# Strassen's products in a weight fold, sums of q one stage earlier, and PSUM split by phase

## The chip, the cores and the metric

One core of one Trainium2 chip. The metric is the device time of one execution in microseconds (us), median of several executions. Times in profile lines count from the start of the span. An execution counts as slow when it lies over 1.5% above the fastest of the same kernel; ratios use the fast ones. One execution of each version keeps a trace; where that is a slow one, the text says so. "The clock" is the clock that was granted to TensorE, as a share of full speed.

## The reference, cut to what matters

```python
q_lm = q.reshape(B, H, 32, S // 32, D).mean(axis=3)      # B, H, S, D = 8, 8, 576, 64
k_lm = k.reshape(B, H, 32, S // 32, D).mean(axis=3)
A, Bm, C = sm(q, k_lm), sm(q_lm, k_lm), sm(q_lm, k)      # softmax of scaled products
Z = Bm^T / (norm1(Bm) * norminf(Bm) + 1e-6)
for _ in range(6):
    Z = 2 * Z - Z @ Bm @ Z
x = (A @ Z @ C @ v)                                      # -> 4608 x 512
h = (x @ w1) * (x @ w2) @ w3                             # w1, w2: 512 x 1024; w3: 1024 x 1024
out = h @ w_out                                          # w_out: 1024 x 512
```

The kernel multiplies w3 by w_out once (the "fold") and so has one product less per token.

## The kernel before

There are two regions. In the first 82.5 us TensorE folds w3 into w_out, with the attention of batch 0 in between. Then come eight rounds, one per batch: an **up** phase (x times w1 and w2, with the next batch's attention woven in by stages) and a **down** phase (times the folded weight, with what is left of that attention, the Newton chain of Z). The attention is a generator; each `yield` ends a stage, and the loop decides where a stage is issued. What is issued on an engine behind a wait comes after it: in the changed kernel TensorE stood 11.2 us for v at L283, and the fold's products issued behind that began only afterwards, at 60.7.

PSUM: three tiles of two banks in turn (`big`), one bank `small`, one bank `acc`.

```python
def big():
    return psp.tile([128, 2, 512], FP32, name="big", bufs=3)
...
def attention(st, bank=None, vbank=None):
    combine(st, 0)                 # lm of q = sum of two halves, on VectorE
    nc.vector.tensor_tensor(out=qbd, ...)               # block diagonal of it
    psB = small()                  # Bm's scores: first use of lm on TensorE
    ...
    yield
    scores_c(0); es0 = presum(0)   # on GpSimd (POOL)
    combine(st, 1)                 # lm of k, used by scores_a two stages on
    yield
    ...                            # Newton: six iterations, then
                y = pz.tile([128, 2, 32], FP32, name="y")
                nc.vector.tensor_tensor(out=y, in0=old[:, :, 2, :], in1=pv_[:, :, 1, :], op=ALU.add)
                ybd = pz.tile([128, 2, 4, 32], FP32, name="ybd")
                nc.vector.tensor_tensor(out=ybd, in0=y..., in1=mask4..., op=ALU.mult)
    ...
    psZ = small()                  # ybd is the moving operand of this product
```

The fold and its loads (order of issue is what matters):

```python
for n, (j, cc) in enumerate(blocks):          # 16 half row blocks of w3
    # transpose four 128x128 pieces on TensorE, copy to SBUF, then
    nc.tensor.matmul(psW[j][:, :], turned[j, cc][:, c4, :], wof[:, c, :], ...)   # 512 columns
...
fd = fold(pf, wof, w3f)
steps(fd, 5)
load_w3(3)
turn_all(0)                                   # transposes of q and k, batch 0
steps(load_v(sts[0], 0), 9)                   # v of batch 0
...
load_weight(0, moe_w1); load_weight(1, moe_w2)
steps(load_qk(sts[1], 1), 9)
```

The softmax here doesn't subtract the row's maximum and nothing guards it: scores larger than these inputs give would overflow.

## Time and profile before

| | kernel before |
|---|---|
| median time | 296.25 us (295.93 to 298.0, 3 runs) |
| profiled span | 293.7 us, of an execution of 295.47 us; granted clock 0.997 |
| first up product (L437) | 82.5 us |
| from there to the end | 211.2 us |
| waits of TensorE for the sums of q (L197) | 2.2 us by the view of waits |

Two stretches make the time: up to the first up product, which I call the **fold region**, and the **rounds** after it.

### The profile page before, as it was taken

The page shows a single profiled execution, that of the slowest core. Times are in us where ns is not written, and L with a number is a line of the kernel's source. Part 1 is how long each engine was busy: PE and PEld are TensorE (multiplying, and loading weights), DVE is VectorE, ACT ScalarE, POOL GpSimd, SP SyncE. Part 2 cuts the span into 40 slices and gives each one's busy share as a digit, 9 for nine tenths or more (in the row PEclk, how much of TensorE's full clock was granted, in tenths as well). Part 3 has the DMA queues.
Part 4 walks back from the last instruction along what each step waited for, and adds up shares of the span by engine and source line. Part 5 has one row for each costly group of instructions (what it writes and reads, how often), then busy time and mean ns, then how long its engine had stood idle before and what let it go on. Part 6 is the DMA issues. An engine that isn't in the chain of part 4 may idle for free.

```text
span 293.7 us, 8702 instructions
## 1 busy us (share of the span) xinstructions
PE 279.8 (95%) x3632; PEld 155.3 (53%) x3632; DVE 168.7 (57%) x416; ACT 127.3 (43%) x209; POOL 130.7 (45%) x157
## 2 busy tenths in 40 slices
PE   7999998989999999999999999999999999999994
PEld 4444454444466546654664565466546645654741
DVE  7111145434048678665876786586678657975620
ACT  1000026994164257225723742474257236625531
POOL 0208805078029906950794299049807910400000
PEclk9999999999999999999999999999999999999998
DMA  6999999999915889896999799979979365003124
GB/s 230 337 251 205 242 261 206 176 215 207 157 27 69 147 260 167 123 254 187 145 133 280 177 147 166 294 137 141 187 230 148 91 164 158 2 21 90 37 52 126
DMA packets 69127, 48.80 MB, mean 166 GB/s; under 512 B 40672, under 2 KB 61152, under 8 KB 69088
## 3 DMA queue, kind: packets, MB, share of 16 engines
q1 hardware_dynamic: 54208, 34.62, 49.3%
q0 software_dynamic: 13792, 11.54, 27.5%
q10 hardware_dynamic: 1088, 2.10, 1.9%
q8 instruction: 28, 0.46, 0.6%
q14 instruction: 11, 0.09, 0.1%
HBM read 38.80 MB, written 9.44 MB: 164 GB/s over the span
## 4 chain that ended last, share of the span: by engine, by line
PE 82%; DVE 7%; ACT 5%; DMA 3%; issue 2%; ACTq 0%; DVEq 0%
PE big L437 20%; PE acc L511 13%; PE acc L457 11%; PE big L457 9%; PE small L511 5%; PE small L273 5%; PE big L423 4%; DVE ab L443 3%; PE small L365 3%; PE acc L365 3%; DMA wof<-in_moe_w_out_dram 3%; DVE gt L429 2%; PE small L399 2%; PE big L479 2%; ACT gt L427 1%
## 5 line engine op out<-in xcount | busy, mean ns | idle before, releaser
L437 PE MATMUL big<-ahat,gt 128*128 128x288 f16 x512 | 74.3, 286 | 0.8
L443 DVE TENSOR_TENSOR ab<-a_sb,big 128x576 f16<-128x576 f16 x64 | 48.1, 752 | 25.1 <-PE big L437 11.3
L441 ACT CAST a_sb<-big 128x576 f16<-128x576 f32 x64 | 40.8, 638 | 37.6 <-PE big L437 37.6
L437 PEld LDWEIGHTS <-gt 128*128 128x128 f16 x512 | 46.5, 97 | 18.2 <-issue 2.2
L511 PE MATMUL acc<-wof,w3t 128*128 128x512 f32 x96 | 46.8, 608 | 2.1 <-ACT w_79 L514 1.1
L457 PE MATMUL acc<-w_79,ab 128*128 128x512 f16 (+1 forms) x192 | 40.9, 381 | 0.0
L457 PEld LDWEIGHTS <-ab 128*128 128x128 f16 (+1 forms) x320 | 24.9, 100 | 29.1 <-issue 7.3
L154 POOL TENSOR_TENSOR tr<-qkT 128x768 f32<-128x768 f16 x16 | 26.4, 1649 | 24.2 <-DMA qkT<-qkn 24.0
L457 PE MATMUL big<-w_79,ab 128*128 128x512 f16 x128 | 32.3, 381 | 0.0
L429 DVE TENSOR_SCALAR gt<-big 128x512 f16<-128x512 f32 x32 | 20.6, 687 | 20.0 <-ACT gt L427 20.0
L463 ACT ACTIVATE o_sb<-acc 128x512 f32<-128x512 f32 x20 | 11.9, 598 | 42.1 <-PE acc L457 41.1
L156 POOL TENSOR_TENSOR tr<-tr,qkT 128x768 f32<-128x768 f32 x16 | 26.4, 1652 | 0.4
L511 PEld LDWEIGHTS acc<-wof,w3t 128*128 128x128 f32 x96 | 16.3, 190 | 16.4 <-issue 11.9
L487 DVE COPY w3t<-big 128x512 f32<-128x512 f32 (+1 forms) x15 | 8.5, 583 | 28.2 <-PE big L479 28.2
L427 ACT ACTIVATE gt<-big 128x512 f16<-128x512 f32 x32 | 17.8, 596 | 6.9 <-PE big L423 6.9
L463 ACT ACTIVATE o_sb<-big 128x512 f32<-128x512 f32 x16 | 9.6, 598 | 21.3 <-PE big L457 20.4
L423 PE MATMUL big<-wdup,zt 128*32 128x512 f16 x256 | 17.6, 382 | 0.8 <-DVE zt L406 0.5
L273 PE MATMUL small<-vt,ect 96*32 96x64 f32 x672 | 15.5, 223 | 0.6 <-issue 0.6
L92 ACT COPY wdup<-wdup 64x1024 f16<-64x1024 f16 x16 | 15.4, 1040 | 0.1
L514 ACT CAST w_79<-acc 128x512 f16<-128x512 f32 x6 | 3.5, 586 | 27.2 <-PE acc L511 27.2
L511 PE MATMUL small<-wof,w3t 128*128 128x512 f32 x32 | 14.7, 593 | 0.0
L221 ACT ACTIVATE ect<-big 96x768 f32<-96x768 f32 x16 | 12.9, 808 | 1.6 <-PE big L217 1.6
(148 smaller groups left out, 342.8 us busy)
## 6 DMA issues: line engine op xcount, KB each, us to landing
vt<-in_v_dram SPq DMA_DIRECT2D x24, 288.0 KB, 4.4
out_dram<-o_sb SPq DMA_DIRECT2D x24, 192.0 KB, 2.6
qkn<-in_q_dram POOLq DMA_DIRECT2D x12, 288.0 KB, 5.7
qkn<-in_k_dram POOLq DMA_DIRECT2D x12, 288.0 KB, 6.1
w3f<-in_moe_w_dram SPq DMA_DIRECT2D x6, 512.0 KB, 8.6
out_dram<-o_sb SPq DMA_DIRECT2D x24, 128.0 KB, 3.4
vt<-in_v_dram SPq DMA_DIRECT2D x2, 1152.0 KB, 9.2
wof<-in_moe_w_out_dram ACTq DMA_DIRECT2D x4, 512.0 KB, 7.7
```

What stands on the lines that cost most here:

```text
L154: nc.gpsimd.tensor_tensor(out=tr, in0=x[:, :, 0, :], in1=x[:, :, 1, :], op=ALU.add)
L156: nc.gpsimd.tensor_tensor(out=tr, in0=tr, in1=x[:, :, 2, :], op=ALU.add)
L273: nc.tensor.matmul(psV[32 * h:32 * h + 32, 0:64], ects[qd][0:NP, h, r, :], vt[0:NP, 4 * qd + h, 64 * r:64 * r + 64], start=(r == 0), stop= ...
L423: nc.tensor.matmul(psG[32 * h:32 * h + 32, n, :], zt[:, 4 * qd + h, :], wdup[:, 4 * qd + h, w, 512 * n:512 * n + 512], start=True, stop=Tr ...
L427: nc.scalar.activation(out=dst[:, 0, :], in_=psG[:, 0, :], func=AXF.Copy, scale=1.0 / ZS)
L429: nc.vector.tensor_scalar(out=dst[:, 1, :], in0=psG[:, 1, :], scalar1=1.0 / ZS, scalar2=None, op0=ALU.mult)
L437: nc.tensor.matmul(p[:, c, 0:HS], st["g"][qd][:, w, 128 * j:128 * j + 128], st["ahat"][qd][:, c, :], start=(qd == 0), stop=(qd == 1))
L441: nc.scalar.copy(out=st["a_sb"], in_=p[:, :, 0:HS])
L443: nc.vector.tensor_tensor(out=st["ab"][:, j, :].rearrange("p (c s) -> p c s", c=2), in0=st["a_sb"], in1=p[:, :, 0:HS], op=ALU.mult)
L457: nc.tensor.matmul(pso[o:o + sz, :], ab[:, j, s0:s0 + sz], w34[:, j, :], start=(j == 0), stop=(j == 7), tile_position=(0, o))
L463: nc.scalar.activation(out=o_sb, in_=pso[:, :], func=AXF.Copy, scale=1.0 / (X64 * X64))
L511: nc.tensor.matmul(psW[j][:, :], turned[j, cc][:, c4, :], wof[:, c, :], start=(c == 0), stop=(c == 7))
```

## The change

Its intent: row blocks 2 to 7 of the fold, in pairs, with Strassen's seven products instead of eight; the sums of q a stage ahead of Bm, so that Bm's scores do not wait; copies of w1 and w2 to the other 64 partitions ("doubling") half on VectorE; the iterations of the Newton chain further apart in the fold (`slots`); and PSUM split so that the fold gets banks of its own and the rounds get `third` and `acc` in their place. To find room, three rows of w3 and the sums of w_out lie in the two buffers of v, so v of batch 0 is loaded later. The diff, cut to its core:

```diff
+    ps_fold = tc.tile_pool(name="psf", bufs=1, space=bass.MemoryType.PSUM)
+    ps_late = tc.tile_pool(name="psl", bufs=1, space=bass.MemoryType.PSUM)
     def big():
-        return psp.tile([128, 2, 512], FP32, name="big", bufs=3)
+        turns["n"] += 1
+        if psl is not None and turns["n"] % 3 == 0 and not turns["held"]:
+            return third()
+        return psp.tile([128, 2, 512], FP32, name="big", bufs=2)
+    def third():
+        return psl.tile([128, 2, 512], FP32, name="third")
@@ attention: a stage boundary behind the sums of q, combine(1) later
+        yield
         psB = small()
         ...
         scores_c(0)
         es0 = presum(0)
-        combine(st, 1)
         yield
         ...
         nc.vector.transpose(out=bt, in_=bm)
+        combine(st, 1)
         yield
@@ fold: rows 0 and 1 as before; sums of w_out; then per pair of rows
+                if n == 2 and c4 == 0:
+                    put(s4, wb[1][0], wb[0][0], ALU.subtract, nc.gpsimd)
+                    put(s1, wb[0][0], wb[1][1], ALU.add, nc.gpsimd)
+                if n == 2 and c4 == 2:
+                    put(s6, wb[0][0], wb[0][1], ALU.add)
+                if n == 3 and c4 == 0:
+                    put(wb[0][1], wb[0][1], wb[1][1], ALU.subtract)
+            for i, (a, rhs) in enumerate(products):          # seven
+                m = psf.tile([128, 256], FP32, name="mm", bufs=2)
+                for c in range(4):
+                    nc.tensor.matmul(m, cur[a][:, c, :], rhs[:, c, :], ...)
+                ...                                          # sums of products on VectorE
@@ loads
+        w3x, sums = (pin.tile([128, H, 384], FP32, name="vt")... for _ in range(2))
         turn_all(0)
-        steps(load_v(sts[0], 0), 9)
         landmarks(sts[0])
         load_weight(0, moe_w1)
         load_weight(1, moe_w2)
         steps(load_qk(sts[1], 1), 9)
         exchange(sts[0], 0)
         exchange(sts[0], 1)
+        steps(fd, 16)
+        load_w3(7)
         for n in range(28):
-            steps(at)
+            if n == 0:
+                steps(load_v(sts[0], 0), 9)
+            if n in slots:
+                steps(at)
-                double_weight(0, 2 * n - 7)
+            if 12 <= n < 20:
+                double_weight(nc.vector.tensor_copy, 1, n - 12)
@@ rounds
+            if n == nd - 4:
+                at = attention(sts[b + 2], acc) if b + 2 < B else iter(())
+                steps(at)
```

## The prediction

> **What bounds the kernel now.** I read the page first (busy times and groups), then the timeline of the first 100 us, then the waits, then the DMA packets. The page:
>
> ```profile
> span 293.7 us, 8702 instructions
> ...
> PE 279.8 (95%) x3632; PEld 155.3 (53%) x3632; DVE 168.7 (57%) x416; ACT 127.3 (43%) x209; POOL 130.7 (45%) x157
> ...
> L511 PE MATMUL acc<-wof,w3t 128*128 128x512 f32 x96 | 46.8, 608 | 2.1 <-ACT w_79 L514 1.1
> ...
> L511 PE MATMUL small<-wof,w3t 128*128 128x512 f32 x32 | 14.7, 593 | 0.0
> ```
>
> PE is busy 95% of the span, and the first fold lines say what the change attacks: w3 times w_out, L511, is 128 PE records for 64 matmuls in the source, since each f32 matmul is two passes. The profiled span is 293.7 us and the timed median 296.25, so I add 2.55 us to a span to get a time.
>
> The timeline gives the true cost of a pass:
>
> ```profile
> 12.09 2.74 PE L511 MATMUL small<-wof,w3t 128*128 128x512 f32 x6
> ...
> 30.16 0.60 PE L479 MATMUL big<-ident,w3f 128*128 128x128 f32 x4
> 30.60 4.46 PE L511 MATMUL small<-wof,w3t 128*128 128x512 f32 x10
> ...
> 60.37 0.61 PE L399 MATMUL small<-ybd,xd 128*128 128x128 f32 x4
> ```
>
> Ten passes take 4.46 us, of which the last shows its full 0.59: (4.46 - 0.59)/9 = 0.430 us from start to start. The fold so holds PE for 128 x 0.430 = 55.0 us, 41.3 of it for row blocks 2 to 7. L399, f32 with 128 columns and a fresh weight load each time, goes at (0.61 - 0.275)/3 = 0.112 us, so a 128x128 f32 weight load can repeat every 0.11 us and stays hidden behind a pass of 256 columns.
>
> Where PE waits, from the groups of waits and from the starts in the timeline:
>
> ```profile
> PEld L197 <- DVE lm L174: 4.1, 6, 0.8
> ...
> PE acc L511 <- ACT w_79 L514: 1.1, 2, 0.9
> ```
>
> L197 (Bm's scores) waits at six stage boundaries for the sums of q. From start to start these are 0.444 us three times and 0.630 three times beyond the work, where a plain change of operation costs 0.093. Over the first 82.3 us the fold and attention 0 lose another 3.1 us in seven waits of 0.2 to 1.05 us, the largest where ACT's copy of w34 (L514) stands behind work of its own queue.
>
> [...] at 16.0 to 17.5 us w3 (4096-byte packets, SP queue) ran at about 305 GB/s and k (768-byte packets, POOL queue) at 52, some 37 packets each per half us; alone, k ran at 203. [...] (L487, 512 f32 columns, 0.69 us; lm, 256 columns, 0.42), and I use those two durations.
>
> **The change, part by part.**
>
> 1. Strassen. 3 pairs x 7 products x 4 matmuls = 84 matmuls of 256 columns, 168 passes x 0.2155 = 36.2 us, in place of 96 x 0.430 = 41.3. PE gains **5.0 us** (7/8, as it should be). The 16 transposed groups stay 16. Added on DVE per pair: five sums of 512 (0.69 each) and eight of 256 out of PSUM (0.42), 6.8 us; 20.5 in all, against 8 copies x 0.69 taken away; three sums of w_out on DVE and two on POOL (1024 columns; L154's 1.65 us for 768 makes about 2.2 each). In 24 to 76 us DVE is under half busy, and the two product banks leave 1.7 us per product, so I count these as hidden, with 0.5 us of small stalls (one bank `tr` for all transposes).
>
> 2. Doubling of wdup half on DVE, and slots further apart for the Newton iterations (two fold steps of 0.86 us between them, before mostly one). This should remove about 2 of the 3.1 us of waits. Up to the end of region A (82.3 us now) I get -5.0 - 2.0 + 0.7 = **-6.3 us** if every load is there in time.
>
> 3. Sums of q one stage ahead: 3 x 0.444 + 3 x 0.630 - 6 x 0.093 = **-2.7 us**. PSUM split: the up phase keeps three buffers in turn, the down phase two plus one; it neither adds nor takes a wait that I can point to. One more iteration falls into the up phase, where `small` is held by the product with v; I give 0.4 us back. So **-2.3**.
>
> 4. The loads. Rows 2 to 4 of w3 now lie in one vt buffer and the sums of w_out in the other. So v of batch 0 can be issued only when the last transpose of row 4 is done. I count PE forward: 16 matmuls of rows 0 and 1 end at about 24.0 us (22.4 now, plus three more transposes of 0.43, plus 0.3); 26 more of 0.431 and four transposes put that point at **36.9 us**. The first use of v (L283, in order on PE) comes 12 fold matmuls, two transposes and three attention stages later: 5.2 + 0.9 + 1.9 = 8.0, at **45 us**. Now v is issued at 23.58 and lands at 31.7, in a quiet stretch. After, it stands in the SP queue behind the exchange of k's sums and row 7 of w3, and beside w1, w2, q and k of batch 1 on the POOL queue, which run from about 34 to 57 us:
>
> ```profile
> vt<-in_v_dram SPq DMA_DIRECT2D x2, 1152.0 KB, 9.2
> ...
> wdup<-in_moe_w_dram POOLq DMA_DIRECT2D x2, 1024.0 KB, 13.9
> qkn<-in_q_dram POOLq DMA_DIRECT2D x2, 576.0 KB, 13.1
> qkn<-in_k_dram POOLq DMA_DIRECT2D x2, 576.0 KB, 15.8
> w3f<-in_moe_w_dram SPq DMA_DIRECT2D x4, 256.0 KB, 6.0
> ```
>
> Packets of v are 1536 bytes (0.091 us each), those of w1 and w2 0.172 us: in turn, 16 x 1536 / 0.263 us = 93 GB/s, and 144 beside q and k. 1.18 MB then takes 8 to 12 us. With row 7 ahead of it until about 42 us (the like load, issued at 34.6 now, lands at 43.5), v lands at an estimated **49 to 54 us**. PE then stands 4 to 9 us at L283, and at the long end loses a further 1 us or so to the clock. Central: **+6.5 us**.
>
> Sum: -6.3 - 2.3 + 6.5 = -2.1, span 291.6, time 294.1; I state **293.5 us**, leaning a little toward the shorter wait, since a tuned schedule would hardly keep the longest.
>
> **The rivals.** (a) v arrives in time, as the slots intend: then -8.6, time about 288. For it: v took 8.2 us in its quiet stretch. Against it: the POOL stream is certain to run at that moment, and row 7 must come first. (b) The wait for v takes nearly the whole 9 us and the clock drops: -8.6 + 10 = about 298. For it: the exchange now issued at 33.25, beside the start of w1, needed until 40.7 to land. Against: PE would meet other waits there anyway. (c) DVE becomes the bound of the fold: some 29 us of fold and sum work beside the Newton chain, in order. Then iterations slip by 0.5 us each and the time is about 296. Against: DVE was busy 4.4 to 5.0 us of each 10 between 40 and 70.
>
> **Range and chances.** Rival (a) with some luck gives the lower end, **289.0**, rival (b) the upper, **298.5**. Faster by over 2% means below 290.3: it needs a wait for v under about 3 us, to which I give 0.2. Slower than 302.2 needs two of the rivals at once, 0.05. Within 2%: **0.75**.
>
> **What would show each step.** Product passes (L574) start to start 0.215 us, 168 of them[...]. A wait of L283 for DMA vt of several us at about 45 us, once, in batch 0 alone; none would make me wrong towards faster. The waits of L207 (Bm's scores) at the six boundaries down to about 0.1 us. The stretch from the first up matmul to the end 2 to 3 us shorter than the 211 now. Granted clock below 1.0 after the wait for v[...]. If the fold ends before 77 us, step 4 failed; if DVE lines end PE's waits in the fold, step 1's "hidden" failed.

## More of the kernel before

The prediction shows the lines of the page; one more group matters later, VectorE's write of `ybd` (columns: count, shortest/median/longest ns, first and last start, forms):

```profile
L377 DVE TENSOR_TENSOR ybd<-y,mask_129 x8: 424/432/611, 59.4 to 264.3; 128x256 f32<-128x256 f32 x8
```

## The result, and the profile after

The changed kernel took **314.05 us** median (309.71 to 316.61, 4 runs), the kernel before on the same chip 296.88. The ratio of the mean of one kernel's fast runs to the mean of the other's in the same rounds is 1.0495, 95% interval 1.036 to 1.063; it is not quite the ratio of the medians, and here it rests on two fast runs, since two of the four are slow. The run with the trace is one of these two (314.55 us, span 312.7; the fast ones have spans of 307.6 and 311.5, and all four a mean clock of 0.971 or 0.972), so the losses below are those of a long run: up to 5 us more than in the fastest. Slower by 5%, where I had said 293.5 and at most 298.5.

The page's first line and two others (second line of each quotation: busy time, share, instructions; third: granted clock in tenths, 40 slices):

```profile
span 312.7 us, 8888 instructions
...
PE 278.5 (89%) x3704; PEld 170.3 (54%) x3704; DVE 197.2 (63%) x458; ACT 121.2 (39%) x203; POOL 138.2 (44%) x159
...
PEclk9999996579999999999999999999999999999999
```

TensorE's busy time hardly fell (279.8 to 278.5), although the products became fewer (3.0 us of it are work at half clock, see below), and the clock row has a hole at slices 7 to 9. The first up product (L448 now) comes at 94.9 us instead of 82.5: **12.4 us lost in the fold region**; from there to the end it is 217.8 instead of 211.2: **6.6 lost in the rounds**. The waits of TensorE (what it waited for: us in total, times, longest):

```profile
PE big L283 <- DMA vt<-in_v_dram: 11.2, 1, 11.2
PE third L269 <- DVE lm L183: 2.7, 7, 0.5
PE small L409 <- DVE ybd L387: 2.5, 4, 1.1
PE small L283 <- issue: 2.4, 2, 1.9
PE tr L499 <- DMA w3f<-in_moe_w_dram: 2.2, 1, 2.2
PE small L375 <- DVE chain L381: 1.5, 1, 1.5
...
PE tr L499 <- DVE aop L512: 1.4, 1, 1.4
```

The first line is the one that the prediction's fourth step named. L207, Bm's scores, is gone from the view, as its third step said; but L269 and L409 have come in its place. The timeline of TensorE and of the queue SP that carries the loads:

```profile
47.86 0.63 PE L499 MATMUL tr<-ident,w3f 128*128 128x128 f32 x4 [2.23 <-DMA w3f<-in_moe_w_dram]
...
59.93 0.87 PE L283 MATMUL big<-vt,ect 96*32 96x64 f32 x24 [11.19 <-DMA vt<-in_v_dram]
```

```profile
39.11 0.53 SPq L624 DMA_DIRECT2D w3f<-in_moe_w_dram  x1
39.74 0.38 SPq L90 DMA_DIRECT2D vt<-in_v_dram  x1
```

Row 7 of w3 was issued at 39.1 and landed at 47.7 (TensorE stood 2.2 us for it), v at 39.7 and landed at 59.8: 12.1 us behind the row before it in its queue. w1 and w2, issued just ahead on POOL's queue, landed at 49.4 and 58.6. After the wait the clock stays down (columns of this view: stretch, length, busy us of PE, PEld, DVE, ACT, POOL with counts, granted clock, DMA share, GB/s):

```profile
59.50:66.00 6.50, 6.07 (x58) 4.34 (x59) 2.30 (x8) 2.36 (x3) 0.00 (x0) 0.50 1.31 181
66.00:70.00 4.00, 4.00 (x67) 2.94 (x70) 2.08 (x6) 4.00 (x6) 1.54 (x1) 0.98 1.24 217
```

6.07 us of work at half clock would have been 3.0 at full, so another 3.0 us are lost; from start to start the passes took 0.426 us until 65.9 and 0.216 after. But the half clock did not begin late in the gap of 11.2 us: the clock was at half from 49.1 us on, 0.4 us into the gap and soon after the wait of 2.2 us for row 7:

```profile
48.70:49.10 0.40, 0.04 (x8) 0.00 (x0) 0.00 (x0) 0.40 (x2) 0.40 (x1) 1.00 1.05 211
49.10:59.90 10.80, 0.00 (x0) 0.00 (x1) 0.00 (x0) 1.61 (x3) 0.28 (x1) 0.50 1.16 217
```

Other traces below have stretches of half clock, 3.4 or 6.8 us long, after single pauses of TensorE of only 1.5 us (unshift), 1.7 and 2.2 (v_early_act), 1.8 (best1) and 2.0 (shift_lm), while a pause of 1.6 in best3 and seven of 1.5 in unshift have none. So half clock follows pauses of 1.5 to 2.2 us in some runs and not in others.

The fold region adds up: v 11.2, clock 3.0, row 7 2.2, and 1.4 and 1.5 for VectorE (L499 and L375 above) are +19.3; less 5.1 for the products, as predicted, and the 3.1 of waits that the kernel before has there, +11.1, of 12.4 measured. (These terms are worked out from the views of one slow run; 1.3 us are not traced to a cause.)

Strassen's products themselves went as predicted: 96 + 72 records of line L574, 0.216 us apart at full clock.

The sums of w_out did not go as predicted. The view of their line (count, shortest/median/longest ns, first and last start, forms):

```profile
L512 POOL TENSOR_TENSOR vt<-wof x2: 2361/2848/3336, 16.5 to 18.8; 128x1024 f32<-128x1024 f32 x2
L512 DVE TENSOR_TENSOR wof<-wof x2: 2358/2808/3257, 20.0 to 27.1; 128x1024 f32<-128x1024 f32 x2
L512 DVE TENSOR_TENSOR vt<-wof x1: 2902/2902/2902, 17.0 to 17.0; 128x1024 f32<-128x1024 f32 x1
```

VectorE took up to 3.3 us for a sum of 1024 columns from SBUF. In a run below with no such overlap it took 1.216. The same holds for its copies in the doubling: 0.41 us for the shortest of eight, 2.20 for the longest, beside an add of POOL.

The same view has a group that tells the operands apart. The three `aop<-aop`, with both operands in SBUF, took 0.68 us twice with no POOL instruction beside them, and 2.11 once beside POOL's adds (32.7 to 34.8); the twelve `aop<-tr,aop`, with one operand in PSUM (`tr`), took 0.675 to 0.692, seven of them beside an add of POOL. And of the eight copies the two beside POOL took 2.20 and 0.98 us, the six with nothing of POOL beside them 0.41 to 0.42. So two operands in SBUF beside POOL looked like what stretches a sum on VectorE. I tested it below.

### The profile page after: what moved, and what is told of

It is laid out like the page before. It is cut to its first block, busy times and chain, and to the rows that moved or that the text cites.

```text
span 312.7 us, 8888 instructions
## 1 busy us (share of the span) xinstructions
PE 278.5 (89%) x3704; PEld 170.3 (54%) x3704; DVE 197.2 (63%) x458; ACT 121.2 (39%) x203; POOL 138.2 (44%) x159
## 4 chain that ended last, share of the span: by engine, by line
PE 54%; DVE 9%; issue 3%; ACT 1%; POOL 0%; DVEq 0%; ACTq 0%
PE big L448 14%; PE acc L468 10%; PE third L468 8%; PE big L434 5%; PE small L283 4%; PE third L448 3%; DVE ab L454 3%; PE acc L375 3%; PE small L409 2%; DVE ybd L387 1%; PE third L269 1%; DVE lm L183 1%; PE big L360 1%; PE small L375 1%; DVE chain L255 1%
## 5 line engine op out<-in xcount | busy, mean ns | idle before, releaser
L448 PE MATMUL big<-ahat,gt 128*128 128x288 f16 x408 | 62.1, 287 | 1.2 <-issue 0.7
L448 PEld LDWEIGHTS <-gt 128*128 128x128 f16 x512 | 45.8, 97 | 16.4 <-issue 1.3
L238 POOL TENSOR_TENSOR t<-ect 96x384 f32<-96x384 f32 x16 | 16.0, 997 | 82.1 <-ACT ect L231 54.5
L468 PE MATMUL acc<-w,ab 128*128 128x512 f16 (+1 forms) x192 | 39.7, 381 | 0.0
L468 PE MATMUL third<-w,ab 128*128 128x512 f16 x128 | 32.2, 380 | 0.0
L574 PE MATMUL mm<-wof,aop 128*128 128x256 f32 x96 | 23.5, 386 | 0.0
L574 PE MATMUL mm<-vt,aop 128*128 128x256 f32 x72 | 20.5, 426 | 0.0
L452 ACT CAST a_sb<-third 128x576 f16<-128x576 f32 x16 | 10.2, 638 | 23.9 <-PE third L448 23.9
L574 PEld LDWEIGHTS mm<-wof,aop 128*128 128x128 f32 x96 | 17.4, 190 | 3.1 <-issue 0.8
L283 PE MATMUL small<-vt,ect 96*32 96x64 f32 x672 | 15.8, 223 | 2.4 <-issue 2.4
L448 PE MATMUL third<-ahat,gt 128*128 128x288 f16 x104 | 17.1, 286 | 0.2 <-ACT o_sb L474 0.2
L554 PE MATMUL big<-wof,aop 128*128 128x512 f32 x32 | 15.3, 599 | 1.0 <-DMA wof<-in_moe_w_out_dram 0.5
```

What stands on the lines that cost most here:

```text
L238: nc.gpsimd.tensor_tensor(out=t3[0:NP], in0=e[:, :, 0:3, :], in1=e[:, :, 3:6, :], op=ALU.add)
L283: nc.tensor.matmul(psV[32 * h:32 * h + 32, 0:64], ects[qd][0:NP, h, r, :], vt[0:NP, 4 * qd + h, 64 * r:64 * r + 64], start=(r == 0), stop= ...
L448: nc.tensor.matmul(p[:, c, 0:HS], st["g"][qd][:, w, 128 * j:128 * j + 128], st["ahat"][qd][:, c, :], start=(qd == 0), stop=(qd == 1))
L452: nc.scalar.copy(out=st["a_sb"], in_=p[:, :, 0:HS])
L468: nc.tensor.matmul(pso[o:o + sz, :], ab[:, j, s0:s0 + sz], w34[:, j, :], start=(j == 0), stop=(j == 7), tile_position=(0, o))
L574: nc.tensor.matmul(m, cur[a][:, c, :], rhs[:, c, :], start=(c == 0), stop=(c == 3))
```

## The experiments

All were run as full kernels that give the correct result. A call of four runs shared one chip and its runs of the kernel before: 296.38 us median for the first four runs below in time order (v_early, unshift, shift_only, v_early_unshift), 296.11 for the next four (v_early_act, v_early_sums, v_early_unshift2, best1), 296.95 for qbd_early, shift_lm, shift_ybd and best2, 296.75 for the last two.

### Was it the load of v?

**v_early**: rows 2 to 4 of w3 lie elsewhere, so v of batch 0 is issued where the kernel before issues it. To make room the rows get a third buffer, and the loads of rows 4 and 5 change places; all else is as in the change.

```diff
-        w3x, sums = (pin.tile([128, H, 384], FP32, name="vt")... for _ in range(2))
+        w3f |= {j: pat.tile([128, DF], FP32, name="gt0", bufs=2) for j in (2, 3)}
+        sums = pin.tile([128, H, 384], FP32, name="vt")...
         ...
         turn_all(0)
+        steps(load_v(sts[0], 0), 9)
         ...
         for n in range(28):
-            if n == 0:
-                steps(load_v(sts[0], 0), 9)
```

> The changed kernel with rows 2 and 3 of w3 in the buffers that later hold gt0, a third buffer for the other rows, and v of batch 0 issued right after the transposes of q and k, as before the change. Theory 'late v': the wait of 11.4 us for v, the half clock after it (about 3.5 us in the trace) and part of the wait for row 7 go, so about 15 us less than the changed kernel: 298 to 300 us. Rival 'DVE of the fold' (the sums on DVE and their collisions with POOL set the pace of the fold): PE then waits for DVE in other places and less than 8 us come back, 306 us or more.

Measured 303.22 us median (301.23 to 309.48), 1.0224 of the kernel before (1.0151 to 1.0296): 10.8 us of the median come back, less than the 15 of my theory and more than the 8 of the rival. The wait of 11.2 us and the half clock are gone (clock 1.00 from 40 to 80 us). The first up product comes at 82.4 instead of 94.9, and the rounds stay at 217.4. So 12.5 us of the fold region hang on this load in the two profiled runs. But 82.4 is the time of the kernel before: the 5.1 us of Strassen are not there either. In their place TensorE waits in that region for:

```profile
PE small L409 <- DVE ybd L387: 4.9, 6, 2.0
PE third L269 <- DVE lm L183: 2.5, 7, 0.4
PE tr L499 <- DMA w3f<-in_moe_w_dram: 1.9, 1, 1.9
...
PE tr L499 <- DVE aop L512: 1.4, 1, 1.4
```

(2.0 us of the first line lie in the fold region, at 68.4; the second line is of the rounds.)

**v_early_act**: the doubling all on ScalarE.

```diff
-            if 12 <= n < 20:
-                double_weight(nc.vector.tensor_copy, 1, n - 12)
+            if 12 < n < 21:
+                double_weight(nc.scalar.copy, 1, n - 13)
```

> v_early with all sixteen doublings of wdup on ACT, one per step. In v_early the stretch up to the first up matmul is 82.2 us, no shorter than before, with waits of PE of 2.2 us ahead of the product with ybd and 1.1 in a Strassen product near 68 to 73 us. Theory 'DVE beside POOL': DVE's operations on two SBUF operands, or its fast copies, stand while POOL works on SBUF (one doubling took 2.2 us against 0.42 alone); without the doublings DVE keeps up, 2 to 3 us come back: 300 us. Rival 'ACT queue': the doublings delay ACT's copies of products and zt, as before the change, and nothing or less than 1 us is won.

302.63 us (298.77 to 304.24), 1.0138 (1.0061 to 1.0215): by the time alone not to be told from v_early, whose interval overlaps. Its profiled run is one of the slow ones, with half clock from 48.5 to 55.4 us and from 181.7 to 185.1, so its spans settle nothing. In its trace the wait for `ybd` in the fold region falls from 2.0 to 0.8 us, and the wait of 0.9 for VectorE at 73.5 is gone.

**v_early_sums**: two edits at once. All four first sums of w_out go to POOL, so that none on VectorE lies beside them, and row 7 of w3 is loaded ahead of the second exchange.

```diff
+                    put(s6, wb[0][0], wb[0][1], ALU.add, nc.gpsimd)
+                    put(wb[0][1], wb[0][1], wb[1][1], ALU.subtract, nc.gpsimd)
                     put(s4, wb[1][0], wb[0][0], ALU.subtract, nc.gpsimd)
                     put(s1, wb[0][0], wb[1][1], ALU.add, nc.gpsimd)
-                if n == 2 and c4 == 2:
-                    put(s6, wb[0][0], wb[0][1], ALU.add)
-                if n == 3 and c4 == 0:
-                    put(wb[0][1], wb[0][1], wb[1][1], ALU.subtract)
         ...
         exchange(sts[0], 0)
-        exchange(sts[0], 1)
         steps(fd, 16)
         load_w3(7)
+        exchange(sts[0], 1)
```

> v_early with four of the five sums of w_out on POOL, one after the other (DVE keeps the last), and row 7 of w3 loaded ahead of the exchange of k's sums. Theory 'DVE beside POOL': two DVE sums took 2.9 and 3.3 us beside POOL's 2.4 and 3.3 where an estimate from L154 and lm gives 1.1 to 2.2; the 1.6 us wait for the fourth transpose of the first pair goes; the wait of 2.0 us for row 7 goes with its earlier load. Together 2.5 to 3.5 us less than v_early: 300 us. If the fold waits for POOL's later sums instead, no gain.

300.33 us (296.58 to 302.52), 1.0107 (1.0027 to 1.0188). Its interval overlaps that of v_early, so by the time alone the gain is not shown, and its profiled run is a slow one. In the trace the waits at 23.8 and 45.6 (1.4 and 1.9 us) are gone, and the first up product comes at 79.9, 2.5 earlier than in v_early, in spite of half clock from 67.8 to 71.2; the wait for `ybd` just before it, at 64.8, grew to 3.1 us, behind two copies of the doubling on VectorE that took 1.63 and 2.39 us beside POOL. The one sum left on VectorE now stands alone:

```profile
L512 DVE TENSOR_TENSOR wof<-wof x1: 1216/1216/1216, 25.4 to 25.4; 128x1024 f32<-128x1024 f32 x1
```

1.216 us against 2.36 to 3.26 in the change. The two edits were not separated.

### The rounds: the shift and the banks

**unshift**: the change without the shift of stages; Strassen, loads and banks as in the change.

```diff
-        yield
         psB = small()
         es0 = presum(0)
+        combine(st, 1)
-            if n == nd - 4:
-                at = attention(sts[b + 2], acc) if b + 2 < B else iter(())
-                steps(at)
+        at = attention(sts[b + 2], acc) if b + 2 < B else iter(())
```

> The changed kernel with the sums of q in one stage with Bm again, combine(1) where it was, and the next attention created at the end of the down phase; Strassen and the PSUM split stay. The part after the fold became 6.4 us longer. Theory 'stage shift': the shift did that (combine(1) behind the chain of bt, ybd beside POOL), so about 6 us come back: 308 us. Rival 'PSUM split': the two plus one buffers did it, and the time stays at 312 to 315 or rises by the 2.7 us that the shift was to gain.

321.17 us (318.7 to 322.73), 1.0833 (1.0776 to 1.0890): slower than the change by 7 us, the opposite of what I looked for. The rounds take 226.6 us, of which some 1.7 go to a stretch at half clock (168.8 to 172.3). Seven times TensorE waits for a bank:

```profile
PE third L467 <- DVE rmix L352: 10.7, 7, 1.5
```

L467 is the first down product into `third`. Without the shift, the denominators of the attention (the tile psS, taken by `big()`, and held until VectorE has made `rmix` of it) come, in the turn of three, to lie in `third` when the down phase begins. Before, the down phase took any of three tiles. So the split of PSUM is not neutral: in this kernel **it needs the shift**. **v_early_unshift** is the same with v early.

> Both: v early and no stage shift, so Strassen and the PSUM split without the two suspected losses. If both theories hold, the 5 us of Strassen and some of the removed waits are seen: 288 to 292 us. If the Strassen sums on DVE eat their gain, 295 to 298.

311.87 us (306.27 to 315.42), 1.0378 (1.0320 to 1.0437); both of my expectations missed. Its profiled run is a slow one, and its trace has the same seven waits with the same sum, 10.7 us. **v_early_unshift2** keeps that one tile out of `third`:

```diff
         def denominators():
-            ps = big()
+            ps = psp.tile([128, 2, 512], FP32, name="big", bufs=2)
```

> v_early without the stage shift, and with the tile of the denominators taken from the two buffers of big, never from third. In unshift PE waited 1.68 us per batch at the first down matmul into third, because the denominators held third. Theory 'the split needs the shift': these waits go, and the part after the fold is 211 us as before the change, so 4 to 6 us less than v_early: 297 to 299 us. Rival 'PSUM split costs by itself': waits move to other buffers and the time stays over 302.

297.35 us (296.97 to 306.48), 1.0045 (0.9997 to 1.0092). The seven waits are gone, and the rounds take 213.2 us against 217.4 with the shift. So, once that bank is free, the version without the shift is faster, by some 4 us in these two traces. Not all of it is the shift's own: 2.9 us of v_early's rounds are the pauses that the view calls "issue", against 0.2 here (more on them under qbd_early). **shift_only** looks at this from the other side: the kernel before with the shift alone.

```diff
+        yield
         psB = small()
         es0 = presum(0)
-        combine(st, 1)
         nc.vector.transpose(out=bt, in_=bm)
+        combine(st, 1)
+            if n == nd - 4:
+                at = attention(sts[b + 2], acc) if b + 2 < B else iter(())
+                steps(at)
```

> The kernel before with the stage shift alone (qbd a stage of its own, combine(1) after bt, attention of the next batch begun four steps before the end of the down phase). Theory 'stage shift': 3 to 6 us slower than before, 300 to 303. Rival 'PSUM split' (and the prediction): 2 to 3 us faster than before, 294.

300.17 us (299.6 to 301.09), 1.0135 (1.0103 to 1.0167). The waits at Bm's scores are gone here as well; in their place stand:

```profile
PE small L400 <- DVE ybd L378: 3.5, 4, 1.3
PE big L260 <- DVE lm L174: 2.9, 8, 0.4
PE big L329 <- issue: 1.8, 1, 1.8
...
PE small L274 <- issue: 1.2, 1, 1.2
```

L260 is scores_a: it waits for the sum of k, which the shift put behind the chain of `bt` on VectorE. L400 is psZ. The two pauses ("issue") in which TensorE waits for nothing that the view names were 0.6 each before.

**shift_lm**: combine(1) ahead of the chain of `bt` again.

```diff
+        combine(st, 1)
         rbs = pz.tile([128, 2], FP32, name="rbs")
         ...
         nc.vector.transpose(out=bt, in_=bm)
-        combine(st, 1)
```

> The kernel before with the stage shift (300.2 us in its run), and combine(1) issued ahead of the bt chain again instead of behind it. Theory 'the new 0.47 to 0.57 us waits at scores_a come from the landmark of k being queued behind the bt chain on VectorE': these seven waits go, sum 3.5 us less, about 297. Rival 'VectorE has no room in that stretch, whatever the order': the waits move to the bt chain or to the psZ product, and the time stays within 1 us of 300.

303.32 us (301.97 to 305.21), 1.0232 (1.0160 to 1.0303): my theory fell. The seven waits at scores_a are gone, and the up product waits instead, seven times, for VectorE's product `ab`:

```profile
PE big L438 <- DVE ab L444: 4.3, 7, 0.6
```

The rival was right that the waits move, but it named other places for them, and a time within 1 us of 300. Some 1.7 us of the profiled run are half clock (210.3 to 213.7, after a pause of 2.0). As far as these two orders show, VectorE has no room in that stretch: its order only chooses who waits. That no order would do is not shown.

**qbd_early**: the kernel before, with the sums of q one step early and every later stage left where it was.

```diff
+        yield
         psB = small()
-            steps(proj if n in (nd - 3, nd - 2) else at)
+            if n != nd - 1:
+                steps(proj if n in (nd - 3, nd - 2) else at)
+            if n == nd - 4:
+                steps(at, 9)
+                at = attention(sts[b + 2], acc) if b + 2 < B else iter(())
+                steps(at)
```

> The kernel before with one thing alone moved: the sums of the two q outputs (landmark, block diagonal) of the batch after next are started one up phase step earlier, behind the fourth step from the end instead of the last; all later stages stay where they are, and so does PSUM. The waits of TensorE at the scores_a transposed product (L197 of the kernel before), 3 of 0.44 and 3 of 0.63 us, sum 3.2, go, and nothing takes their place, because combine(1), the Bm sums and the bt chain are not moved. Theory 'the waits are only moved by what the change shifted along': about 2.6 us less, 293.5. Rival 'any shift of the q sums collides with the fold phases or the y chain': within 0.5 us of before, with the waits elsewhere.

299.63 us (299.49 to 301.29), 1.0122 (1.0055 to 1.0188): both expectations missed. The waits of 3.2 us are gone, and the kernel is slower all the same. psZ waits 1.6 us, and one of TensorE's pauses is 3.4 us instead of 0.6, with half clock from 126.0 to 129.4 after it, which is another 1.7 us. These two are 4.4 us over the kernel before, and the span is 4.0 longer (297.7): by this estimate the early sums themselves neither cost nor gain much here. The timeline:

```profile
125.31 0.16 PE L279 MATMUL small<-ones,es 96*32 96x1 f32 x1 [3.36 <-issue]
```

The traces do tell where these pauses stand. The page counts packets that carry instructions (`q8 instruction: 28, 0.46, 0.6%` in the kernel before: 28 packets, 0.46 MB), and the packet records of the trace give the time of each. The 16 traces have 30 pauses over 0.5 us that the view calls "issue". Each ends 1.1 to 1.7 us after such a packet of 16384 bytes has landed; and where this is the k-th packet of the run, the instruction after the pause is TensorE's number 256 k + 193 or 194, in all 30 cases. So, by these counts, TensorE stands there for the instructions that the packet brings, 256 to a packet; the pauses are 0.55 to 3.36 us long. Here the packet began at 122.5 us, in the kernel before at 120.1. What makes a packet late I did not test.

**shift_ybd**: shift_only, with `y` written into PSUM, so that the write of `ybd` has one operand from SBUF and one from PSUM.

```diff
-                y = pz.tile([128, 2, 32], FP32, name="y")
+                y = psI[:, 128:192].rearrange("p (a m) -> p a m", m=32)
```

> The kernel before with the stage shift, and the product y written into PSUM, so that the block-diagonal write ybd has one operand from SBUF and one from PSUM instead of two from SBUF. Theory 'the write of ybd is stretched to 1 us and over because it reads two SBUF operands while POOL adds landmarks': its longest falls from 1.85 to below 0.8 us, the waits at psZ (up to 1.07 us, sum about 4) fall below 0.4 each, and the time is about 297.5. Rival 'it is only late, by the queue in front of it': its duration falls little, or the waits stay, and the time stays at 300.

298.35 us (296.33 to 301.3), 1.0037 (0.9966 to 1.0108), against 1.0135 (1.0103 to 1.0167) of shift_only: the intervals just touch. The rounds took 211.4 us against 214.7 in the two profiled runs; 1.1 of these 3.3 us are a shorter "issue" pause (0.8 for 1.8). The group of the write in shift_only, then here:

```profile
L378 DVE TENSOR_TENSOR ybd<-y,mask x8: 425/660/1849, 60.8 to 267.6; 128x256 f32<-128x256 f32 x8
```

```profile
L378 DVE TENSOR_TENSOR ybd<-small,mask x8: 424/424/425, 60.8 to 264.3; 128x256 f32<-128x256 f32 x8
```

From 425 to 1849 ns down to 424 to 425: the instruction is the same, only the place of one operand moved. And the timeline of shift_only at one of the long ones, POOL then VectorE:

```profile
156.18 1.65 POOL L156 TENSOR_TENSOR tr<-tr,qkT 128x768 f32<-128x768 f32 x1
```

```profile
156.81 1.31 DVE L378 TENSOR_TENSOR ybd<-y,mask 128x256 f32<-128x256 f32 x1
```

POOL's add ends at 157.83, VectorE's write at 158.12. The other two long ones (1.85 and 1.33 us) end 0.28 and 0.29 us after an add of POOL as well, and so do the two of 1.18 and 1.50 us in the change (0.30 and 0.29). That fits a wait until the other is done; work queued in front of the write, the rival, would not tie its end to POOL's. The waits at psZ, 3.5 us in shift_only, are gone from shift_ybd's view of waits.

### A version without the waits

**best1**: all of the above together on the change: v early, four sums on POOL, row 7 ahead of the exchange, the doubling on ScalarE, no shift, psS never in `third`.

> All of it: v early, row 7 early, four sums of w_out on POOL, doublings on ACT, no stage shift, denominators never in third. If the theories hold, the stretch up to the first up matmul falls from 82.2 to about 76 us and the rest stays at 211: 288 to 291 us, faster than both kernels. If 295 or more, another cost of Strassen is still unfound.

296.75 us (294.27 to 298.92), 1.0000 (0.9935 to 1.0066): the case "295 or more" of the expectation. The first up product comes at 74.7 us: 7.8 us gained, Strassen's 5.1 and most of the waits of the fold region. Then the rounds took 222.4. The profiled run is one called slow, so I take its waits as signs only; one is of a kind that had not been there:

```profile
PE small L282 <- DMA vt<-in_v_dram: 3.6, 1, 3.6
```

It is v of batch 1, whose buffer the sums of w_out hold, issued at 76.2 behind the exchanges and landed at 84.3. The fold, now faster, got to it before its load: the same mistake as with batch 0, uncovered by the gain, and again with half clock after it (83.7 to 90.5; the mean of 80 to 90 is 0.68).

**best2** loads that v ahead of the exchanges, starts each up phase with the same turn of the banks, and takes the sums of q one step early as in qbd_early.

```diff
                 landmarks(sts[1], load_qk(sts[2], 2, 4))
+                steps(load_v(sts[1], 1), 9)
                 exchange(sts[1], 0)
                 exchange(sts[1], 1)
-                steps(load_v(sts[1], 1), 9)
                 ...
-        turns["held"] = False
+        turns.update(n=0, held=False)
```

> The change with v of batch 0 ahead of w1 and w2, four sums of w_out on POOL, row 7 of w3 ahead of the exchange, the doubling on ScalarE, the three psS tiles kept out of the bank of the denominators, v of batch 1 loaded ahead of the exchanges of the first batches, and the q sums one step early with the later stages where they were before. The 3.75 us wait for v of batch 1 after the fold goes, so the 7.8 us that the fold gained are kept; the scores_a waits (3 us) go as well. Theory 'the Strassen fold is worth its products once nothing waits for a load': 287 to 290 us. Rival 'the clock gives it back': the span's granted clock is below 0.98 and the time is 293 to 297, with waits as short.

290.97 us (289.33 to 295.45), 0.9792 (0.9727 to 0.9858), clock 0.999. The wait for v is gone, and the first up product stays at 74.8. It beats both kernels: the interval lies below 1, though not wholly below 0.98. **best2_noq** asks whether the early sums of q have a part in that; it is best2 without them.

> The version of 291.0 us without its last part: the q sums stay where the kernel before has them. Theory 'the gain of the fold is kept by loading v of batch 1 ahead of the exchanges': the span's first up product comes at 74.5 us as in the best version, the 3.75 us wait for v is gone, the waits at the scores_a transposed product are back (3.2 us), time 291 to 293. Rival 'the early q sums are the gain': 295 to 297, as the version without either had (296.75).

290.33 us (289.49 to 294.14), 0.9783 (0.9735 to 0.9831): none. The waits for the sums of q are back and the time is the same. Loading v of batch 1 earlier (together with the reset of the turn, not separated from it) makes the difference to best1.

**best3** is best2 with `y` in PSUM, the edit of shift_ybd.

> The version of 291.0 us with the product y written into PSUM, so that the block-diagonal write ybd reads one operand from SBUF and one from PSUM. Theory 'that write is slowed by POOL's adds because it reads two SBUF operands': its longest falls below 0.8 us, the waits at psZ (5 of 0.3 to 0.57 us, sum about 2.2) go for the most part, time 289 to 290. Rival 'what is left of them is other work queued on VectorE': waits and time as in the best version, 291.

287.59 us (287.16 to 291.41), **0.9743** (0.9663 to 0.9824), 9.2 us below the kernel before in the medians. That it is faster than best2 is not shown, for the intervals overlap; in the traces the waits at psZ (1.3 us in best2) are gone, beside others that the edit does not touch. Its page, and its first waits:

```profile
span 285.4 us, 8891 instructions
...
PE 274.7 (96%) x3704; PEld 169.0 (59%) x3704; DVE 183.6 (64%) x448; ACT 127.6 (45%) x211; POOL 140.8 (49%) x161
```

```profile
PE big L338 <- issue: 1.6, 1, 1.6
PE big L634 <- DVE warm L631: 1.5, 1, 1.5
```

TensorE is busy 5.1 us less than before, the size of Strassen's seven for eight (5.0 predicted), and now the span shows it: the first up product at 74.8 (82.5 before), the rounds 210.6 (211.2). No wait for a load is left among the first, and `ybd` takes 423 to 424 ns every time.

The region numbers of the profiled runs together (the change's is a slow run too):

| run | first up product, us | rounds, us | median time, us |
|---|---|---|---|
| before | 82.5 | 211.2 | 296.25 |
| the change | 94.9 | 217.8 | 314.05 |
| v_early | 82.4 | 217.4 | 303.22 |
| v_early_unshift2 | 82.2 | 213.2 | 297.35 |
| best1 (profiled slow) | 74.7 | 222.4 | 296.75 |
| best2 | 74.8 | 214.1 | 290.97 |
| best2_noq | 75.1 | 212.6 | 290.33 |
| best3 | 74.8 | 210.6 | 287.59 |

## Why the prediction was wrong

It was wrong in size and in direction: 293.5 us said, 314.05 measured; slower by over 2% had been given 0.05.

- **Step 4, the load of v: mechanism right, term mis-sized.** The prediction had +6.5 us, with 9 us and "a further 1 us or so" of clock at its long end. Measured: 11.2 us and 3.0 us of clock, and with the load moved back 12.5 us of the fold region are gone (v_early). The slip is in the landing, "49 to 54": v took 12.1 us from the landing of row 7, the top of the 8 to 12 that I had estimated, but row 7 landed at 47.7 and not at "about 42". Its load was no slower than "the like load" before (8.6 us against 8.9); it was issued late, at 39.1. In its queue it stands behind the exchange of k's sums, and POOL had these sums ready at 37.9, where the kernel before has them at 32.7:

```profile
37.06 0.81 POOL L169 TENSOR_TENSOR parts<-parts,tr 128x256 f32<-128x256 f32 x1
```

```profile
31.91 0.80 POOL L160 TENSOR_TENSOR parts<-parts,tr 128x256 f32<-128x256 f32 x1
```

POOL began its sums 4.0 us later (26.7 against 22.7; k had landed at 24.3 against 20.3, with more rows of w3 loading beside it; whether they delayed it I did not test), and two of its adds took 2.5 and 2.0 us for 1.6. I had kept the times of this queue from the kernel before. That TensorE came to L283 at 48.7 and not at 45 was luck and hid 3.7 us of it. Nor did I ask what a row 7 that late does to its own user: TensorE waited 2.2 us for it. And I named the clock, but the 1 us that I gave it was an estimate that no trace then at hand showed; at half clock for 6 us it is 3.
- **Step 1, Strassen: the products right, "hidden" wrong.** The 168 passes ran 0.216 us apart at full clock, and the 5 us are real in best3. But I counted the sums of w_out at 2.2 us each, from POOL's adds, with three on VectorE and two on POOL, as if the engines did not meet. They slowed each other (up to 3.3 us on VectorE, which alone takes 1.2), and a wait of 1.4 us for VectorE ended in the transposes of the first pair. The test that the prediction itself gave, "if DVE lines end PE's waits in the fold, step 1's 'hidden' failed", came out so.
- **Step 2, the doubling: failed in the same way.** Copies on VectorE took up to 2.2 us beside POOL's sums of k and q, in front of the Newton chain in VectorE's queue; in v_early this is the wait of 2.0 us at 68.4. In the changed kernel's own trace it is the wait of 1.5 us for the chain (L375), with copies of 2.20 and 0.98 us just ahead of it on VectorE. What the step was to take away in waits came back there.
- **Step 3, the shift: the waits that it named are gone, the gain is not.** I predicted -2.3 us in the rounds; they became 6.6 us longer. I subtracted a wait without asking what else moved: combine(1) went along, behind the chain of `bt`, and scores_a waits 2.7 us for it; the last product of the Newton chain came to stand beside POOL's adds, and psZ waits 2.5. The change's "issue" pauses are longer as well (3.1 us in three, 1.2 in two before). shift_only has all of these without Strassen, at +3.8 us.
- **"It neither adds nor takes a wait that I can point to", of the PSUM split: wrong.** The split as it was made, without the shift, adds 10.7 us of waits (unshift), and one line takes them away (v_early_unshift2); in the change it is the shift that hides them. The two parts of the change are not to be judged one by one.
- **The rivals.** Rival (b), that the wait takes nearly all and the clock drops, was the nearest, and still too small. I added the costs of step 4 to gains that were not there. Rival (c), VectorE as the bound, was half right: not by its share of busy time, but by single operations stretched beside POOL.
- **Smaller slips.** The span of 293.7 us belongs to an execution of 295.47, so 1.8 us are to be added to a span and not 2.55; the sum of the parts would have been 293.4. And `lm`, whose 0.42 us I took for the sums of 256 columns out of PSUM, reads two SBUF tiles (`parts` and `other`); those sums took 0.40 to 0.42 us all the same (`c<-c,mm` in the change). The 0.2155 us for a pass of 256 columns was an estimate of mine, close to half of the measured 0.430; the change's trace shows 0.216.

What stays open: what makes a block of TensorE's instructions come late (pauses of 0.6 us before, up to 3.4 in other versions); why half clock follows a pause of 1.5 to 2.2 us in some runs only; 1.3 us of the fold region and part of the 6.6 of the rounds; whether the kernel before would gain from the better order of loads and sums without Strassen, which was not run, so that of best3's 7.7 us in the fold region only the 5.1 of TensorE's busy time are shown to be Strassen's.

## What to carry to other kernels

When a change puts new data into a buffer that a load uses, work out when that load is now issued, what is ahead of it in its queue and beside it on the others, and follow whatever is ahead of it back to what releases it: here the load in front was as fast as before, but 4.5 us later. When it moves a stage to remove a wait, list what else is in the queue of the engine behind it, since the wait may move: in shift_lm the 2.9 us at scores_a went, and 4.3 us came at the up product. And before work is put on VectorE beside POOL, count its operands in SBUF: moving one into PSUM was one line, and brought a write of up to 1.85 us to 0.42 every time.
